# Pairing row blocks 0 and 1 in the second mixing layer of an FNet + GEGLU kernel

## The chip, the cores and the metric

The kernel runs on one core of a Trainium2 chip (trn2). The metric is the device time of one execution in microseconds (us). TensorE (PE in the profile) does the matrix products, VectorE (DVE) and ScalarE (ACT) the elementwise work, GpSimd (POOL) and SyncE (SP) mostly issue DMAs. Hardware behaviour is told here as the traces of this case show it.

## The reference

Four residual layers work on an activation `x` of 2048 rows by 512 columns, in float32. Layers 0 and 2 mix, layers 1 and 3 are a gated feed-forward network:

```
def mix(x):                     # x: 2048 x 512
    a = x @ dft_hid_re.T
    b = x @ dft_hid_im.T
    return dft_seq_re @ a - dft_seq_im @ b

def ffn(x):
    return (gelu(x @ w_gate) * (x @ w_up)) @ w_down     # 1792 hidden columns

x = x + mix(layernorm(x)); x = x + ffn(layernorm(x))    # layers 0 and 1
x = x + mix(layernorm(x)); x = x + ffn(layernorm(x))    # layers 2 and 3
```

All weights are inputs that don't change between the layers: layers 0 and 2 use the same sequence matrices.

## The kernel before

**Products.** A float32 tile is split into a high and a low part (`split`, L122: ACT copies the high part in a rounded type at L124, DVE subtracts it from the source at L126), and one product of tiles is three matrix instructions, high by high, high by low and low by high (`mm3`, L162, lines 164 to 166), summed in PSUM. Each has a 128x128 stationary and a 128x512 moving operand. In the feed-forward layers and in the sequence product of the mixing layers, the matrices are divided into two by two blocks and multiplied in Winograd's form of Strassen's algorithm: seven block products (A11, A12, S1, S2, S3, S4, A22 by their left operand) in place of eight, for sums and differences of blocks that DVE makes (`minus` L151, `plus` L154).

**The mixing layers** (`mix`, L711) multiply the sequence matrices with the normalized rows first, for four row blocks `b` of 512 output rows (`NB` is 4), and the hidden matrices then. `plan` (L403) writes out the order of a layer's stages. Layer 0 begins with the first two products of all four row blocks in one pass (`fore`); layer 2 does them one row block after the other (`a11`, `a12`). They are followed, for each row block, by stages S2 (`s2`, L823: three block products, 8 steps each) and S4 (`s4`, L859: two block products). A step (`six`, L752) takes one tile of the sequence matrices and issues six matrix instructions. The results of a row block are eight tiles of sums, `cs`. Then one of two things is done with the hidden matrices:

- `hid_groups` (L729): eight groups of twelve matrix instructions, in three parts that lie between and behind S2 and S4 (`EARLY_HID`, `MID_HID`, `LATE_HID`). Residual rows are added in `x_add` (L204). This is 96 instructions for a row block.
- `pair_products` (L897): two row blocks together are a two by two problem and are multiplied in Winograd's form: seven products of four tiles (`PAIR_ORDER`, L401) by six instructions, 168 for both. `pair_member` (L885) collects the sums of both and loads their residual rows into two wide tiles (`load_turned`, L227); `prepared` (L902) makes the block sums and splits, `LEAD_PAIR` (4) products ahead; `ended` (L926) adds a finished product to the wide tiles (`turned_rows`, L234: a transpose and an addition on DVE) and stores rows (`rows_done`, L244, four DMAs on POOL). The block sums of the hidden matrices for it (`whd`, L262) are made in layer 1.

`PAIRED` (L43) says which row blocks begin a pair: in layer 2 only block 2 (with 3). Blocks 0 and 1 of layer 2, and all of layer 0, go through `hid_groups`.

**The stream.** Every tile of a matrix that is needed in order is an item of `items` (L286). `take` (L315) hands out the next; it splits items up to `AHEAD` (7) before their use, and `split_next` (L308) loads up to `RAW` (6) items before that, all by DMAs of SP. In stage S2 an item loads three tiles of the sequence matrix, and `make_s2` (L345) makes S1, S2 and S3 of them on DVE; S1 and S3 are split by later items, S2 is kept until `make_s4` (L367) has made S4 with it.

**Slots.** Tiles live in 93 slots of 128x512 (`Slots`, L83; `sb.get` and `sb.put`). Two wide tiles, "x" and "z", are lent to the slots as four more each when they are free (`lend` L170, `reclaim` L109); in layer 2 "z" is taken back in S4 of block 0 and "x" in S4 of the block that begins a pair, and nothing may lie in a lent slot when `load_turned` takes the wide tile (L230).

**Other work** is queued: `step` (L486) runs one entry of `queue` after each step of products, and an entry of None is a pause. `chores_at(b)` (L714) is such work for the next layer: for b = 1 and 2 it normalizes the rows of blocks 0 and 1 for layer 3, which it reads back from memory (`x_load_mixed`, L195, four DMAs of SP for 128 rows), and for b = 2 in layer 0 it also makes weights. The scheduler of the framework then sets each engine's order of instructions from a model of the times.

**Start and end.** `WARM` (12, L29) products of an identity matrix (L1320) are issued before the first data; each is two records in the trace. `last_rows` (L1247) does the last block product of the kernel in two cuts of 256 columns, and after each cut it stores four pieces, each issued on an engine of a list (L1253).

Of the kernel before, what the change touches and what calls it, by code (L numbers as in the profile page):

```python
# [9 lines left out]
F32 = mybir.dt.float32  # L10
# [4 lines left out]
P = 128  # L15
# [4 lines left out]
TB = 512  # L20
NB = S // TB
# [6 lines left out]
RAW = 6  # L28
WARM = 12  # L29
OPEN_MORE = 0  # L30
# [10 lines left out]
CUT = 256  # L41
KEEP22 = {0: (2, 3), 2: ()}
PAIRED = {0: (), 2: (2,)}  # L43
NEAR_PAIR = 8
LEAD_PAIR = 4
WHD_AT = 6
BACK_AT = 4, 7
KEEP_AT = 2
# [11 lines left out]
def fnet_geglu(ctx: ExitStack, tc: tile.TileContext, x_in, ws, wh, whc, wgu, wdc, out):  # L60
# [22 lines left out]
    class Slots:  # L83


        def __init__(self, pool, name, n):
            self.pool, self.name, self.free, self.held = pool, name, list(range(n)), {}
            self.least, self.lent = n, set()

        def get(self, dtype=F32):  # L90
            at = next(i for i, n in enumerate(self.free) if dtype == F32 or isinstance(n, int))
            n = self.free.pop(at)
            self.least = min(self.least, len(self.free))
            t = self.pool.tile([P, 512], dtype, name=f"{self.name}{n}") if isinstance(n, int) else n[0]
            self.held[id(t)] = (n, t)
            return t
# [59 lines left out]

    def copied(src):
        v = sb.get()
        nc.scalar.activation(v, src, AF.Copy)  # L159
        return v  # L160
# [92 lines left out]

    def fetched(key):
        t = sb.get()
        nc.sync.dma_start(t, away.pop(key))
        return t
# [86 lines left out]

    def make_s2(k, keep):  # L345
        def run(a21, a22, *a11):
            a11 = a11[0] if a11 else held.pop(k)
            s1 = a22
            if keep:
                held["A22", k], s1 = a22, sb.get()  # L350
            plus(s1, a21, a22)
            minus(a21, a11, a21)
            minus(a11, s1, a11)
            s1s[k], s2s[k], s3s[k] = s1, a11, a21
            return split_slot(a11)
        return run
# [9 lines left out]

    def make_s4(k):  # L367
        def run(a12):
            v = s2s.pop(k)
            minus(a12, a12, v)  # L370
            sb.put(v)
            return plain(a12)
        return run
# [59 lines left out]
    def mix_items(layer):  # L433
# [3 lines left out]
        for b, what in plan(layer):  # L437
# [14 lines left out]
            elif what == "S2":  # L452
                for i, k in skewed(3):
                    if i == 0:
                        raw(make_s2(k, b in KEEP22[layer]), a21[k], a22[k], *(() if hold else (a11[k],)))
                    else:
                        raw(make_s1(k) if i == 1 else make_s3(k))
            elif what == "S4":
                for i, k in skewed(2):
                    if i == 0:  # L460
                        raw(make_s4(k), a12[k])
                    elif b in KEEP22[layer]:
                        raw(make_a22(k))
                    else:
                        raw(plain, a22[k])
# [245 lines left out]
    def mix(layer):  # L711
        hid, sums, chores, hid_left = {}, {}, [], [0]

        def chores_at(b):  # L714
# [46 lines left out]
        def based(b, c, ps):  # L761

            if b >= FORE[layer]:
                return copied(ps)
            v = sb.get()
            plus(v, sums[b][c], ps)
            return v
# [11 lines left out]
        def a12(b):  # L779
# [4 lines left out]
            for c in range(2):  # L784
                v = sums[b][c]
                if b < FORE[layer]:
                    t = sb.get()
# [35 lines left out]
        def s2(b):  # L823
# [10 lines left out]
            for i, k in skewed(3):  # L834
                if b and fore and i == 0 and k == (0 if layer else BACK_AT[0]):
                    sums[b] = [fetched((layer, b, c)) for c in range(2)]
                if b and fore and i == 0 and k == (0 if layer else BACK_AT[1]):
                    cs.update({(0, c): fetched((layer, b, c, "sum")) for c in range(2)})
                if i == 0:
# [12 lines left out]
                for c in range(2):  # L852
                    if i == 1:
                        v = cs[1, 2 + c] = sb.get()
                        plus(v, us[b][c], one[c])
# [3 lines left out]
        def s4(b):  # L859
# [7 lines left out]
            for i, k in skewed(2):  # L867
# [6 lines left out]
                for c in range(2):  # L874
                    if i == 0:
                        v = cs[0, 2 + c] = sb.get()
                        plus(v, u[c], one[c])
# [7 lines left out]
        def pair_member(b):  # L885

            if b in PAIRED[layer]:
                pair.update({(0, key): cs.pop(key) for key in list(cs)})
                queue.extend([run for chore in chores_at(b) for run in (chore, None)])
            elif b - 1 in PAIRED[layer]:  # L890
# [6 lines left out]
        def pair_products(b):  # L897

            bs, ys, banks, seconds = {}, {}, {}, {}
            chores.extend(chores_at(b))  # L900

# [45 lines left out]
            for i, (name, k) in enumerate(PAIR_ORDER):  # L947
# [113 lines left out]
    def geglu(w, layer):  # L1061
# [185 lines left out]
        def last_rows():  # L1247
# [216 lines left out]
```

## Time and profile before

| What | Value |
|---|---|
| Median of 3 runs | 1597.19 us (1595.58 to 1597.57) |
| The profiled execution's own time | 1594.87 us |
| Its span, first to last instruction | 1593.1 us |
| Outside the span | 1.77 us |
| TensorE's mean granted clock | 0.999 |
| TensorE busy | 1585.2 us |
| VectorE busy | 1245.9 us |
| ScalarE busy | 865.0 us |
| GpSimd busy | 233.4 us |
| DMA | 418.66 MB, mean 263 GB/s |

The profiled execution is one run. It was 2.32 us below the median of the three timed runs, so a sum over its rows gives a difference, and the difference is carried over to the median. Busy times are shares of one engine's own line; TensorE's are of matrix instructions that overlap (each shows 388 ns on average, but one starts well before the one ahead of it has ended), so the distance between starts is what one instruction costs.

The times of the stages can be read off by counting matrix instructions along TensorE's line. Layer 0 lies at about 6.5 to 398 us: the common pass to 94, then 76 us for each row block, so that block 2 has 246 to 322 us. Layer 1 lies at 398 to 798 us, layer 2 at 798 to 1184: the first products to 885, blocks 0 and 1 at 885 to 961 and 961 to 1037, S2 and S4 of blocks 2 and 3 at 1037 to 1146, their pair at 1146 to 1184. Layer 3 takes the rest. The scheduler lets neighbouring stages overlap a little, so these bounds are rough.

### The profile page before, as it was taken

Reading aid. Unit: us, or ns where it says so; the run is one execution under the profiler, and the core shown is the slowest. Engines: PE = TensorE matmul, PEld = TensorE weight load, DVE = VectorE, ACT = ScalarE, POOL = GpSimd, SP = SyncE. Lnnn points to the kernel's source line nnn. Section 1 sums busy time; section 2 is a strip of 40 time slices with the busy share of each in tenths; the row PEclk is TensorE's granted clock in tenths of the full one; section 3 lists DMA queues with packets and bytes.
Section 4 is the critical chain, followed back from the end, with each engine's and each line's share of the span. In section 5 each row is a group of like instructions: output and inputs, shape, how many; then the busy total and the mean of one; then the engine's idle time right before and its main releaser. Section 6 shows DMA issues by size and latency. Waiting matters only on the chain.

```text
span 1593.1 us, 23069 instructions
## 1 busy us (share of the span) xinstructions
PE 1585.2 (100%) x7026; PEld 1313.6 (82%) x7026; DVE 1245.9 (78%) x2164; ACT 865.0 (54%) x1696; POOL 233.4 (15%) x410
## 2 busy tenths in 40 slices
PE   9999999999999999999999999999999999999998
PEld 8888888888888888888888888888888888888887
DVE  8999989798799794666869978788985458754475
ACT  7864565544766653656767535446446435433361
POOL 2200311302455201230031000001002000000000
PEclk9999999999999999999999999999999999999999
DMA  9946967897999989995867687768998967896452
GB/s 361 332 146 231 376 225 240 285 300 256 327 344 337 307 304 300 313 338 200 298 225 253 233 272 250 238 228 248 271 352 237 285 201 237 298 282 200 137 191 55
DMA packets 249500, 418.66 MB, mean 263 GB/s; under 512 B 28608, under 2 KB 81856, under 8 KB 248352
## 3 DMA queue, kind: packets, MB, share of 16 engines
q1 hardware_dynamic: 224720, 334.07, 65.5%
q0 software_dynamic: 23840, 82.73, 14.2%
q8 instruction: 56, 0.92, 0.2%
q10 hardware_dynamic: 816, 0.39, 0.1%
q14 instruction: 68, 0.56, 0.1%
HBM read 335.54 MB, written 81.53 MB: 262 GB/s over the span
## 4 chain that ended last, share of the span: by engine, by line
PE 85%; issue 11%; DMA 3%; SPq 0%; POOL 0%; ACT 0%; POOLq 0%; DVE 0%
PE p L164 28%; PE p L165 28%; PE p L166 28%; DMA s<-ws 1%; DMA s<-wb 1%; DMA wide<-x 1%; DMA out<-wide 0%; POOL out L245 0%; SPq L300 0%; SPq L232 0%; SPq L192 0%; SPq L1048 0%; ACT s L124 0%; ACT s L556 0%; POOLq L1460 0%
## 5 line engine op out<-in xcount | busy, mean ns | idle before, releaser
L165 PE MATMUL p<-s,s 128*128 128x512 f32 (+1 forms) x2334 | 902.7, 388 | 0.0
L166 PE MATMUL p<-s,s 128*128 128x512 f32 (+1 forms) x2334 | 890.8, 388 | 0.0
L164 PE MATMUL p<-s,s 128*128 128x512 f32 (+1 forms) x2334 | 879.5, 388 | 0.2 <-ACT s L124 0.2
L124 ACT ACTIVATE s<-s 128x512 fp32r<-128x512 f32 (+1 forms) x848 | 476.6, 607 | 326.1 <-DVE s L152 112.9
L126 DVE TENSOR_TENSOR s<-s,s 128x512 fp32r<-128x512 f32 (+1 forms) x848 | 531.8, 662 | 56.7 <-ACT s L124 49.3
L164 PEld LDWEIGHTS p<-s,s 128*128 128x128 f32 x2334 | 438.4, 188 | 91.4 <-ACT s L124 1.4
L165 PEld LDWEIGHTS p<-s,s 128*128 128x128 f32 x2334 | 438.4, 188 | 90.4 <-DVE s L126 0.6
L166 PEld LDWEIGHTS p<-s,s 128*128 128x128 f32 x2334 | 438.2, 188 | 89.9 <-DVE s L126 0.3
L155 DVE TENSOR_TENSOR s<-s,p 128x512 f32<-128x512 f32 x284 | 190.8, 683 | 195.0 <-PE p L166 111.8
L152 DVE TENSOR_TENSOR s<-s,s 128x512 f32<-128x512 f32 (+1 forms) x411 | 246.9, 617 | 4.8 <-DMA s<-ws 2.5
L159 ACT ACTIVATE s<-p 128x512 f32<-128x512 f32 x246 | 143.7, 592 | 144.8 <-PE p L166 140.2
L1058 ACT ACTIVATE s<-s 128x512 f32<-128x512 f32 x112 | 70.4, 629 | 120.5 <-DVE s L155 110.2
L283 POOL DMA_DIRECT2D wb<-s x84 | 46.0, 549 | 118.9 <-ACT s L124 81.9
L124 ACT ACTIVATE s<-xwide 128x512 fp32r<-128x512 f32 (+1 forms) x68 | 41.0, 616 | 34.9 <-DVE xwide L155 7.2
L1072 DVE TENSOR_TENSOR s<-s,s 128x512 f32<-128x512 f32 x84 | 57.8, 689 | 1.9
L126 DVE TENSOR_TENSOR s<-xwide,s 128x512 fp32r<-128x512 f32 (+1 forms) x68 | 45.2, 676 | 6.9 <-ACT s L124 6.9
L556 ACT ACTIVATE s<-s,shift,rstd 128x512 f32<-128x512 f32 x54 | 43.1, 807 | 4.1 <-DVE shift L520 4.0
L245 POOL DMA_DIRECT2D out<-wide x8 | 5.2, 657 | 271.6 <-DVE wide L155 181.0
L155 DVE TENSOR_TENSOR s<-s,s 128x512 f32<-128x512 f32 (+1 forms) x70 | 41.0, 588 | 4.9 <-DMA s<-ws 3.2
L283 POOL DMA_DIRECT2D wc<-s x42 | 30.3, 723 | 73.3 <-ACT s L124 50.6
L529 POOL TENSOR_SCALAR rstd<-rstd 128x1 f32<-128x1 f32 x48 | 12.8, 268 | 191.3 <-ACT junk L528 190.4
L245 POOL DMA_DIRECT2D x<-wide x12 | 7.9, 662 | 215.3 <-DVE wide L155 214.4
(107 smaller groups left out, 530.7 us busy)
## 6 DMA issues: line engine op xcount, KB each, us to landing
s<-ws SPq DMA_DIRECT2D x367, 256.0 KB, 4.9
s<-wb SPq DMA_DIRECT2D x294, 256.0 KB, 5.3
s<-wc SPq DMA_DIRECT2D x196, 256.0 KB, 4.5
wb<-s POOLq DMA_DIRECT2D x98, 256.0 KB, 5.0
s<-wh SPq DMA_DIRECT2D x64, 256.0 KB, 4.8
s<-x SPq DMA_DIRECT2D x53, 256.0 KB, 5.2
xwide<-ws SPq DMA_DIRECT2D x49, 256.0 KB, 4.1
wc<-s POOLq DMA_DIRECT2D x49, 256.0 KB, 5.3
```

The lines of the kernel that those rows point to most:

```text
L124: nc.scalar.activation(hi, src, AF.Copy)
L126: nc.vector.tensor_tensor(lo, src, f32(hi), op=ALU.subtract)
L152: nc.vector.tensor_tensor(out, a, b, op=ALU.subtract)
L155: nc.vector.tensor_tensor(out, a, b, op=ALU.add)
L159: nc.scalar.activation(v, src, AF.Copy)
L164: nc.tensor.matmul(ps, ah, bh, start=start, stop=False, skip_group_check=True)
L165: nc.tensor.matmul(ps, ah, bl, start=False, stop=False, skip_group_check=True)
L166: nc.tensor.matmul(ps, al, bh, start=False, stop=stop, skip_group_check=True)
L283: nc.gpsimd.dma_start(to, t)
L556: nc.scalar.activation(z, x, AF.Identity, bias=shift, scale=rstd)
L1058: nc.scalar.activation(t, g, AF.Gelu_apprx_tanh)
L1072: nc.vector.tensor_tensor(t, t, v, op=ALU.mult)
```

## The change

Row blocks 0 and 1 of layer 2 become a pair as well, so the stages of the layer are now S2 and S4 of blocks 0 and 1, their pair, S2 and S4 of blocks 2 and 3, and their pair. While a layer has block 0 in a pair, the tiles of sums (`cs` and what leads to them) are taken from the 93 own slots only and never from lent ones (`own=True` and `strict`), and the wide tile "x" is taken back in S4 of block 0. The work for layer 3 that used to lie in the hidden products of block 1, and behind S4 of block 2, is queued behind the first pair, 6 pauses first (`PAIR_WAIT`) and 3 pauses after each entry (`PAIR_GAP`).

The sequence matrices are the same in layers 0 and 2, so layer 0 now also writes the block sums S1, S2, S3 and S4 of row block 2 to memory (`stored_for`: 4 tiles for each of 8 steps, 32 DMAs of 256 KB on POOL's queue), and layer 2 reads them there: stages S2 and S4 of block 2 load as many tiles as before and have no sums to make.

One warming product goes, and the lists of issuing engines of the two last cuts are exchanged in part.

```diff
-WARM = 12
+WARM = 11
...
-PAIRED = {0: (), 2: (2,)}
+PAIRED = {0: (), 2: (0, 2)}
+PAIR_GAP = 3
+PAIR_WAIT = 6
+STORED = 2,
...
-            self.least, self.lent = n, set()
+            self.least, self.lent, self.strict = n, set(), False
...
-            at = next(i for i, n in enumerate(self.free) if dtype == F32 or isinstance(n, int))
+            at = next(i for i, n in enumerate(self.free) if dtype == F32 and not (own and self.strict) or isinstance(n, int))
...
+    stored = {(b, k, n): dram.tile([P, 512], F32, name=f"{n}_{b}_{k}") for b in STORED for k in range(NK) for n in ("S1", "S2", "S3", "S4")}
+
+    def stored_for(b, k, **tiles):
+
+        if b in STORED:
+            for name, t in tiles.items():
+                nc.gpsimd.dma_start(stored[b, k, name], t)
...
             s1s[k], s2s[k], s3s[k] = s1, a11, a21
+            stored_for(b, k, S1=s1, S2=a11, S3=a21)
             return split_slot(a11)
...
             minus(a12, a12, v)
+            stored_for(b, k, S4=a12)
...
-                    if i == 0:
-                        raw(make_s2(k, b in KEEP22[layer]), a21[k], a22[k], *(() if hold else (a11[k],)))
+                    if layer and b in STORED:
+                        raw(plain, stored[b, k, ("S2", "S1", "S3")[i]])
+                    elif i == 0:
+                        raw(make_s2(b, k, b in KEEP22[layer]), a21[k], a22[k], *(() if hold else (a11[k],)))
...
-                    if i == 0:
-                        raw(make_s4(k), a12[k])
+                    if i == 0 and layer and b in STORED:
+                        raw(plain, stored[b, k, "S4"])
+                    elif i == 0:
+                        raw(make_s4(b, k), a12[k])
...
+        sb.strict = 0 in PAIRED[layer]
...
                 pair.update({(0, key): cs.pop(key) for key in list(cs)})
-                queue.extend([run for chore in chores_at(b) for run in (chore, None)])
+                if 0 not in PAIRED[layer]:
+                    queue.extend([run for chore in chores_at(b) for run in (chore, None)])
...
-            chores.extend(chores_at(b))
+            if b == NB - 1:
+                chores.extend(chores_at(b))
...
+            if b == 1:
+                queue.extend([None] * PAIR_WAIT + [run for at in (1, 2) for chore in chores_at(at) for run in (chore, *[None] * PAIR_GAP)])
...
-            for cut, engines in ((slice(0, CUT), (nc.sync, nc.scalar)), (slice(CUT, TB), (nc.sync, nc.scalar, nc.gpsimd))):
+            for cut, engines in ((slice(0, CUT), (nc.gpsimd, nc.sync, nc.scalar)), (slice(CUT, TB), (nc.sync, nc.scalar))):
```

The other edits pass `own=True` where the tiles of sums are made (`copied`, `based`, `fetched`, `a12`, `s2`, `s4`).

More of the change, by code (lines that the diff above doesn't have):

```diff
@@ L87, in __init__, with get @@
             self.pool, self.name, self.free, self.held = pool, name, list(range(n)), {}
-            self.least, self.lent = n, set()
-        def get(self, dtype=F32):
-            at = next(i for i, n in enumerate(self.free) if dtype == F32 or isinstance(n, int))
+            self.least, self.lent, self.strict = n, set(), False
+        def get(self, dtype=F32, own=False):
+            at = next(i for i, n in enumerate(self.free) if dtype == F32 and not (own and self.strict) or isinstance(n, int))
             n = self.free.pop(at)
@@ L155, in plus, with copied @@
         nc.vector.tensor_tensor(out, a, b, op=ALU.add)
-    def copied(src):
-        v = sb.get()
+    def copied(src, own=False):
+        v = sb.get(own=own)
         nc.scalar.activation(v, src, AF.Copy)
@@ L252, in put_away, with fetched @@
         sb.put(t)
-    def fetched(key):
-        t = sb.get()
+    def fetched(key, own=False):
+        t = sb.get(own=own)
         nc.sync.dma_start(t, away.pop(key))
@@ L343, in make_a11, with make_s2 @@
         return run
-    def make_s2(k, keep):
+    stored = {(b, k, n): dram.tile([P, 512], F32, name=f"{n}_{b}_{k}") for b in STORED for k in range(NK) for n in ("S1", "S2", "S3", "S4")}
[3 more added lines that the diff above has]
+                nc.gpsimd.dma_start(stored[b, k, name], t)
+    def make_s2(b, k, keep):
         def run(a21, a22, *a11):
@@ L365, in make_s3, with make_s4 @@
         return lambda: plain(s3s.pop(k))
-    def make_s4(k):
+    def make_s4(b, k):
         def run(a12):
@@ L763, in based @@
             if b >= FORE[layer]:
-                return copied(ps)
-            v = sb.get()
+                return copied(ps, True)
+            v = sb.get(own=True)
             plus(v, sums[b][c], ps)
@@ L786, in a12 @@
                 if b < FORE[layer]:
-                    t = sb.get()
+                    t = sb.get(own=True)
                     plus(t, v, side[c])
@@ L837, in s2 @@
                 if b and fore and i == 0 and k == (0 if layer else BACK_AT[1]):
-                    cs.update({(0, c): fetched((layer, b, c, "sum")) for c in range(2)})
+                    cs.update({(0, c): fetched((layer, b, c, "sum"), True) for c in range(2)})
                 if i == 0:
@@ L853, in s2 @@
                     if i == 1:
-                        v = cs[1, 2 + c] = sb.get()
+                        v = cs[1, 2 + c] = sb.get(own=True)
                         plus(v, us[b][c], one[c])
@@ L875, in s4 @@
                     if i == 0:
-                        v = cs[0, 2 + c] = sb.get()
+                        v = cs[0, 2 + c] = sb.get(own=True)
                         plus(v, u[c], one[c])
```

## The prediction

> **What bounds the kernel now.** I read the page first, then TensorE's groups by shape, its waits and a piece of its timeline, then the windows of the stages, and the two ends last. The page:
>
> ```profile
> span 1593.1 us, 23069 instructions
> PE 1585.2 (100%) x7026; PEld 1313.6 (82%) x7026; DVE 1245.9 (78%) x2164; ACT 865.0 (54%) x1696; POOL 233.4 (15%) x410
> DVE  8999989798799794666869978788985458754475
> ```
>
> TensorE is busy in 1585.2 of 1593.1 us. Busy alone does not prove the bound, since the records overlap, so the waits come next:
>
> ```profile
> PE p L1321 <- POOL ident masks.py:199: 1.4, 1, 1.4
> PE p L164 <- ACT s L124: 0.2, 1, 0.2
> ```
>
> These two rows are all that TensorE waited for: 1.4 us ahead of the warming products and 0.2 us once later. Two rows of its timeline, with 43 starts from the one to the other, give its pace:
>
> ```profile
> 1043.14 0.39 PE L165 MATMUL p<-s,s 128*128 128x512 f32 x1
> ...
> 1052.88 0.39 PE L164 MATMUL p<-s,s 128*128 128x512 f32 x1
> ```
>
> (1052.88 - 1043.14) / 43 = 0.2265 us from start to start. The groups by shape say how many there are (the other two lines of `mm3` have 2306 as well):
>
> ```profile
> L165 PE MATMUL p<-s,s 128*128 128x512 f32 x2306 | 894.8, 389 | 0.0
> ```
>
> 3 x 2306 x 0.2265 = 1567 us: the span is this count times this pace, with some 26 us of warming, narrower products, small waits and ends. One wide matrix instruction less is worth 0.2265 us as long as nothing else comes to bound. The windows show what could: their columns are the stretch, its length, the busy time of PE, PEld, DVE, ACT and POOL, the granted clock, the DMA share and GB/s.
>
> ```profile
> 6.50:94.00 87.50, 87.29 (x383) 71.70 (x383) 84.85 (x202) 70.55 (x134) 15.93 (x23) 1.00 0.90 323
> 246.00:322.00 76.00, 76.00 (x337) 62.94 (x336) 65.49 (x112) 43.18 (x86) 20.09 (x37) 1.00 0.80 277
> 885.00:1037.00 152.00, 152.00 (x672) 125.91 (x671) 127.44 (x208) 67.10 (x127) 6.37 (x14) 1.00 0.74 249
> 1146.00:1184.00 38.00, 38.00 (x169) 31.46 (x169) 38.00 (x65) 19.02 (x34) 0.00 (x0) 1.00 1.05 346
> ```
>
> The reader is to see that TensorE is full in every stage, that VectorE is full as well in the pair (38.00 of 38.00), and that the DMA engines are full there too (share 1.05).
>
> **The change, part by part.**
>
> *Products.* Blocks 0 and 1 lose 2 x 96 = 192 instructions of `hid_groups` and gain 7 x 4 x 6 = 168 of the same 128x512 shape. 24 x 0.2265 = **5.44 us** off the engine that sets the end. The clock in all windows is 1.00, so no other pace is to be expected.
>
> *VectorE at the pair.* A pair costs DVE 16 differences, 28 splits, 6 additions and 8 transposes with 8 additions: 66 instructions. The splits of the stream's next 7 items fall beside it too: 73. DVE's own pace, from two rows of its timeline:
>
> ```profile
> 1164.57 3.09 DVE L126 TENSOR_TENSOR s<-s,s 128x512 fp32r<-128x512 f32 x5
> 1167.58 0.68 DVE L148 SCALAR_TENSOR_TENSOR s<-s,s 128x512 fp32r<-128x512 f32 x1
> ```
>
> 3.01 / 5 = 0.602 us each. 73 x 0.602 = 43.9 us stand against 168 x 0.2265 = 38.1 us of products, 5.9 us more. The stretch ahead has to bring that as a lead. S2 and S4 of one block are this window:
>
> ```profile
> 1037.00:1092.00 55.00, 55.00 (x244) 45.56 (x243) 48.80 (x80) 22.92 (x40) 2.24 (x4) 1.00 0.67 214
> ```
>
> 80 x 0.602 = 48.2 us against 240 x 0.2265 = 54.4 us. Over both blocks and the pair DVE has 2 x 48.2 + 43.9 = 140.3 us to do in 2 x 54.4 + 38.1 = 146.9 us, 96%. The window 6.5 to 94 had 84.85 of 87.50, 97%, and TensorE lost 0.2 us there; the pair of blocks 2 and 3 had DVE at 100% and TensorE lost nothing. In the pair's own order the work just fits: the last tile's products begin 6 instructions ahead of the end, at 36.7 us, DVE owes 62 instructions (37.3 us) by then, and the first five tiles are prepared before the pair begins. I take **0**, with 5.9 us as the other end if no lead exists. Below nothing is excluded, since TensorE can't go under its count. Behind the pair, block 2 is lighter than before: its 32 sums are gone (32 x 0.602 = 19.3 us of DVE), which pays for the transposes of the norms moved there. As TensorE bounds, that relief is worth nothing of itself.
>
> *Stores in layer 0.* 32 x 256 KB = 8.39 MB more on POOL's queue in block 2's 76 us. What moves there now, from the DMA view of 246 to 322 us (the second row has 40 slices):
>
> ```profile
> GB/s 218 182 415 365 106 172 229 57 157 279 354 376 273 202 298 260 352 430 224 170 209 212 317 303 364 396 410 418 406 424 223 272 197 396 111 41 235 223 432 361
> DMA packets 9727, 21.04 MB, mean 277 GB/s; under 512 B 1408, under 2 KB 1920, under 8 KB 9465
> ...
> q1 hardware_dynamic: 7673, 13.10, 54.1%
> q0 software_dynamic: 2048, 7.87, 26.0%
> ...
> s<-ws SPq DMA_DIRECT2D x24, 256.0 KB, 5.2
> wh<-s POOLq DMA_DIRECT2D x16, 256.0 KB, 5.8
> ```
>
> ```profile
> L283 POOL DMA_DIRECT2D wh<-s x16 | 9.0, 561 | 33.0 <-ACT s L124 14.0 <-ACT mean L527 10.8 <-DVE s L126 7.9
> ```
>
> 21.04 + 8.39 = 29.43 MB. At the 418 GB/s that single slices reach this takes 70.4 us of the 76; at the 346 GB/s mean of the pair's window it takes 85.1, 9.1 us too many. The traffic that TensorE needs is SP's, 13.10 MB or 172 GB/s, under half of either rate; the stores only hold slots longer, by the 5.8 us to landing of POOL's other stores. I take **0** and keep 9.1 us as the other end. The Trainium skill, "DMA: Bandwidth & Descriptors", section "Where 436 GB/s comes from", says that the side of the HBM, about 358 GB/s, binds such transfers; by it the 29.43 MB would take 82.2 us, 6.2 too many (an estimate from that page), and the trace speaks against it with nine slices over 390 GB/s. The stores' issue is about 32 x 0.561 = 18 us (the last row's mean) on a POOL that is busy for 20.09 of 76 us; behind them wait only its small norm steps and other stores.
>
> *Work for layer 3, and SP's queue.* Rows of block 0 leave last: four DVE instructions (2.4 us), four stores on POOL, their landing. The nearest rows are those stores in layer 3 and their landing, and what SP has waited for rows so far:
>
> ```profile
> 1387.06 2.63 POOL L245 DMA_DIRECT2D out<-wide  x4 [90.65 <-DMA s<-wb]
> ```
>
> ```profile
> DMA to landing us min/median/max: 3.7/6.6/7.9
> ```
>
> ```profile
> SPq L201 <- DMA x<-wide: 9.0, 3, 6.8
> ```
>
> 2.4 + 2.6 + 7.9 = 12.9 us after the pair's last product; the six pauses last 6 x 6 x 0.2265 = 8.2 us. SP can stand for 4.7 us, with the stream's loads queued behind it. Those run up to 7 + 6 = 13 items ahead, 13 x 6 x 0.2265 = 17.7 us, and SP stood 6.8 us for this reason before while TensorE waited for none. **0**; up to 4.7 if the lead is used up.
>
> *Slots.* Eight sums of block 0 stay through block 1's S2 and S4, and the four slots of "x" are gone there. Loads then start later, since they wait for a slot. That stretch shows such waits already, as DVE waiting for a load:
>
> ```profile
> DVE s L155 <- DMA s<-ws: 7.0, 2, 3.8
> ```
>
> It ended no wait of TensorE, so **0**; where these 7.0 us come on top of DVE's 140.3, it is 0.4 us over its 146.9, and its part is in the rival below. The hidden products' loads (32 tiles) give way to 28 tiles, which changes little.
>
> *Start.* The identity products and the chain of waits at the start:
>
> ```profile
> 1.35 5.49 PE L1321 MATMUL p<-ident 128*128 128x128 f32 x24 [1.35 <-POOL ident masks.py:199]
> ```
>
> ```profile
> 4.49 5.13 DMA s<-ws
> 9.64 5.40 DMA s<-ws
> 15.06 5.39 DMA s<-ws
> ...
> 23.64 0.50 PE p L164
> ```
>
> A product less frees TensorE 5.49 / 12 = 0.46 us earlier. But the chain up to 23.64 us is one of loads, so the first products only wait longer there: **0**, at most 0.46 gained.
>
> *End.* The last cut's stores:
>
> ```profile
> 1587.78 0.84 SPq L1263 DMA_DIRECT2D out<-xwide  x2
> 1587.78 0.37 ACTq L1263 DMA_DIRECT2D out<-xwide  x1
> 1588.04 0.58 POOL L1263 DMA_DIRECT2D out<-xwide  x1 [5.32 <-DVE xwide L155]
> ```
>
> ```profile
> out<-xwide SPq DMA_DIRECT2D x2, 128.0 KB, 2.7
> out<-xwide ACTq DMA_DIRECT2D x1, 128.0 KB, 2.9
> out<-xwide POOLq DMA_DIRECT2D x1, 128.0 KB, 3.4
> ```
>
> POOL's lands last, at 1588.04 + 3.4 = 1591.4. In its place ACT issues a second one at 1587.78 + 0.37 = 1588.15, landing near 1591.1. **0.3 us** gained; from 0 to 0.5.
>
> Sum against the profiled execution: 1594.87 - 5.44 - 0.3 = 1589.1 us (a span near 1587.4). The median of the runs shown is 2.32 us above that execution; from it, 1597.19 - 5.7 = **1591.5 us**.
>
> **The rivals.**
>
> 1. *VectorE becomes the bound at the first pair.* Without a lead the pair loses up to 5.9 us: 1591.5 + 5.9 = 1597.4; half of it gives 1594.4. For it: 96% over 147 us without a break, where the hidden products of block 0 (96 instructions in 21.7 us beside 12 of DVE in 7.2) used to give DVE time to catch up, and tighter slots. Against it: the pair of blocks 2 and 3, into which 22 instructions of the next layer's work are queued as well (14 splits, 8 differences), ran without a loss.
> 2. *The stores fill the DMA engines in layer 0* (slower than before). If 346 GB/s is all there is and the loads share the delay, TensorE ends block 2 up to 9.1 us late: 1591.5 + 9.1 = 1600.6. It decides against the change from a delay of 5.7 us on. For it: the pair's window with share 1.05. Against it: loads need 172 GB/s, and the highest slices show room. The figure of the Trainium skill named above (358 GB/s, "DMA: Bandwidth & Descriptors") is the milder form of this rival: with 6.2 us it would end at 1597.7, an estimate from that page, and its chance is within this rival's.
> 3. *SP's queue stands for the rows of block 0*, 4.7 us: 1596.2. Against it: the 6.8 us stood before without a loss.
> 4. *The change doesn't do what it says*: the 24 instructions go, but the time passes to a wait that comes due later, at the head of layer 3, since its norms now begin a pair later. They still end in block 2, with block 3 and a pair (about 92 us) ahead of layer 3, so I give it no price of its own.
>
> **How the numbers follow.** The forecast has 0.75, rival 1 0.13, rival 2 0.06, rival 3 with what remains 0.06. About 0.2% (3.2 us) is what a measurement here can tell from no change, so faster means below 1594.0. The forecast lies there; of rival 1, evenly spread from 0 to 5.9 us, about 0.4 (0.05) does. Rivals 1 and 3 give same for the rest (0.14), rival 2 slower in most of its cases (0.05), same in the others. Faster 0.80, same 0.15, slower 0.05. The range: downwards the start's 0.46 and the end's other 0.2, and the 1.6 us by which the fastest of the three runs lies under the median, 1591.5 - 2.3 = 1589.2; upwards to the part of rival 1 up to 3.5 us, 1595.0. That leaves out the worst of rivals 1 and 3 and rival 2, under 2 in 10.
>
> **What would show it.** Right: 24 fewer wide instructions (8 fewer in each of the three lines), the same 0.2265 us pace, TensorE's waits still under 1 us beside the start, the last landing a few tenths earlier behind the last product. Rival 1: TensorE waits for DVE's L126 or L148 near 1000 to 1035 us. Rival 2: waits for loads or splits at 250 to 330 us, with loads taking well over 5.2 us to land. Rival 3: SP waiting for `x<-wide` at about 1040 us and TensorE with it. The prediction is wrong if any of these adds more than 2.5 us.

## The result, and the profile after

The changed kernel takes 1590.96 us (median of 6 runs, 1590.40 to 1592.87), the kernel before 1596.51 (6 runs, 1595.58 to 1597.57): a ratio of 0.9968 with a 95% interval of 0.9958 to 0.9979, 5.5 us less. Forecast were 1591.5 and 5.7 us less. Against the larger set of runs of before that came with the experiments (28 runs, median 1595.93) it is 5.0 us less. The interval of the ratio says how well the saving is known: it lies between 3.4 and 6.7 us.

The page of the changed kernel, the lines that answer to those of before:

```profile
span 1589.3 us, 23178 instructions
PE 1579.5 (99%) x7000; PEld 1308.4 (82%) x7000; DVE 1249.1 (79%) x2174; ACT 875.8 (55%) x1714; POOL 252.5 (16%) x443
DVE  8999989889799795566969997868985458754475
```

Line numbers moved: L164 to L166 are L167 to L169 now, the split's L124 and L126 are L127 and L129, `minus` and `plus` are L155 and L158. One of the three lines of `mm3` in the groups by shape, and all that TensorE waited for:

```profile
L168 PE MATMUL p<-s,s 128*128 128x512 f32 x2298 | 891.1, 389 | 1.2 <-DVE s L129 1.2
```

```profile
PE p L1343 <- POOL ident masks.py:199: 1.3, 1, 1.3
PE p L168 <- DVE s L129: 1.2, 1, 1.2
PE p L167 <- ACT s L127: 1.2, 3, 0.5
```

2298 stands where 2306 stood: 3 x 8 = 24 instructions fewer, as counted. But the last two rows are new: 2.4 us of waits, where before had 0.2. Of them 0.9 lie in the common pass of layer 0, the others at 919 and 1101 us. The prediction had named waits under 1 us as a sign of being right, and this sign is not met. The windows of the stages that the change touched, with the columns of the earlier fence:

```profile
246.00:322.00 76.00, 76.00 (x337) 62.94 (x336) 64.73 (x111) 43.32 (x86) 28.73 (x54) 1.00 0.98 350
...
994.00:1032.00 38.00, 38.00 (x169) 31.48 (x168) 33.88 (x57) 19.21 (x35) 0.00 (x0) 1.00 0.77 242
1032.00:1086.00 54.00, 54.00 (x240) 44.72 (x239) 36.81 (x62) 39.17 (x90) 13.23 (x25) 1.00 0.95 290
1086.00:1140.00 54.00, 52.78 (x233) 43.38 (x232) 53.97 (x91) 27.82 (x49) 1.13 (x2) 1.00 0.97 279
```

The rows are layer 0's block 2, and in layer 2 the first pair, S2 and S4 of block 2, and S2 and S4 of block 3. The reader is to see three things. The DMA share of layer 0's block 2 went from 0.80 to 0.98. VectorE isn't full in the new pair (33.88 of 38). It is full in block 3 (53.97 of 54), and there TensorE has its one wait of some length: it stands idle for 1.22 us and loses about 1.5 us of its pace.

The difference of the two profiled executions adds up. The spans differ by 3.8 us. 24 x 0.2265 = 5.4 less for the products; 0.4 less between the end of the last product and the end of the span (6.3 before, 5.9 after); 0.5 more up to the end of layer 0's common pass; 1.5 more for the time lost behind it, at 919 us (0.6) and 1101 us (1.5) against 0.6 in all before: -5.4 - 0.4 + 0.5 + 1.5 = -3.8. The medians differ by more because the profiled execution of before, 1594.87, lies below all six timed ones.

### The profile page after: what moved, and what is told of

Same layout as the page of the kernel before. It is cut to its first block, busy times and chain, and to the rows that moved or that the text cites. A ratio compares the mean times of both kernels' runs of the same rounds, so it can differ in the third digit from the quotient of the medians.

```text
span 1589.3 us, 23178 instructions
## 1 busy us (share of the span) xinstructions
PE 1579.5 (99%) x7000; PEld 1308.4 (82%) x7000; DVE 1249.1 (79%) x2174; ACT 875.8 (55%) x1714; POOL 252.5 (16%) x443
## 4 chain that ended last, share of the span: by engine, by line
PE 97%; DMA 1%; DVE 1%; SPq 0%; issue 0%; ACT 0%; POOL 0%; DVEq 0%; ACTq 0%
PE p L168 32%; PE p L167 32%; PE p L169 32%; DMA s<-ws 1%; DVE s L129 0%; ACT s L127 0%; DVE s L155 0%; SPq L303 0%; SPq L195 0%; ACT s L573 0%; DVE wide L155 0%; DVE s L158 0%; DVE xwide L155 0%; POOL rstd L536 0%; DVE s L242 0%
## 5 line engine op out<-in xcount | busy, mean ns | idle before, releaser
L168 PE MATMUL p<-s,s 128*128 128x512 f32 x2326 | 899.0, 388 | 1.2 <-DVE s L129 1.2
L169 PE MATMUL p<-s,s 128*128 128x512 f32 x2326 | 887.4, 388 | 0.0
L167 PE MATMUL p<-s,s 128*128 128x512 f32 x2326 | 871.6, 388 | 1.3 <-ACT s L127 1.2
L127 ACT ACTIVATE s<-s 128x512 fp32r<-128x512 f32 (+1 forms) x868 | 487.6, 608 | 319.3 <-DVE s L155 110.7
L129 DVE TENSOR_TENSOR s<-s,s 128x512 fp32r<-128x512 f32 (+1 forms) x868 | 543.7, 664 | 56.7 <-ACT s L127 52.0
L167 PEld LDWEIGHTS p<-s,s 128*128 128x128 f32 x2326 | 436.6, 188 | 93.1 <-ACT s L127 3.6
L169 PEld LDWEIGHTS p<-s,s 128*128 128x128 f32 x2326 | 436.8, 188 | 89.5
L158 DVE TENSOR_TENSOR s<-s,p 128x512 f32<-128x512 f32 x289 | 194.1, 683 | 196.5 <-PE p L169 119.0
L155 DVE TENSOR_TENSOR s<-s,s 128x512 f32<-128x512 f32 (+1 forms) x414 | 248.5, 619 | 2.9 <-DMA s<-ws 1.0
L127 ACT ACTIVATE s<-xwide 128x512 fp32r<-128x512 f32 (+1 forms) x52 | 31.0, 614 | 26.8 <-DVE xwide L158 10.5
L158 DVE TENSOR_TENSOR s<-s,s 128x512 f32<-128x512 f32 (+1 forms) x68 | 39.9, 587 | 4.7 <-DMA s<-wgu 2.6
L129 DVE TENSOR_TENSOR s<-xwide,s 128x512 fp32r<-128x512 f32 (+1 forms) x52 | 34.7, 675 | 5.9 <-ACT s L127 5.7
```

Source lines behind the costliest of these rows:

```text
L127: nc.scalar.activation(hi, src, AF.Copy)
L129: nc.vector.tensor_tensor(lo, src, f32(hi), op=ALU.subtract)
L155: nc.vector.tensor_tensor(out, a, b, op=ALU.subtract)
L158: nc.vector.tensor_tensor(out, a, b, op=ALU.add)
L167: nc.tensor.matmul(ps, ah, bh, start=start, stop=False, skip_group_check=True)
L168: nc.tensor.matmul(ps, ah, bl, start=False, stop=False, skip_group_check=True)
```

## The experiments

The theory to test was the prediction's: the saving is TensorE's count times its pace, and everything else is hidden. Its rivals were VectorE at the first pair, the stores in layer 0, and the wait for the rows of block 0. "Against the change" below is the difference of a kernel's ratio and the change's 0.9968, times 1596 us; each ratio's interval is about 0.001 (1.6 us) to either side, so such a difference is known to about 2.2 us.

One thing has to be known to read the profiles that follow. Each is one execution, and executions differ in stages that no edit touched. Count TensorE's products from the start, and compare the time of the one that begins at 885 us in the change, behind the first products of layer 2. It comes at the same time in `dve24`, 0.8 us later in `more24`, 1.1 in `store_only`, 1.5 in `gap0`, 1.6 in `gap2`, 2.0 in `hole`, 2.4 in `less24`, 2.7 in `no_store`, 2.8 in `dve32_b2` and 3.7 in `hole2`. In the kernels among these whose edit lies in layer 2 behind this point (all but `store_only` and `no_store`), every engine has the same operations on the same tiles in the same order up to there, buffer numbers apart, so a new order by the scheduler is not the cause; what is stays open. "In place" below means that this part is taken off the profile's difference.

### Are the 24 products the saving?

`store_only` takes the first pair back and keeps the rest of the change:

```diff
-PAIRED = {0: (), 2: (0, 2)}
+PAIRED = {0: (), 2: (2,)}
```

> The changed kernel without the first pair (blocks 0 and 1 go through the hidden products again), with stores, one warming product less and the exchanged ends kept. The 24 instructions are back: if they are the gain, 1591.0 + 5.4 = 1596.4, 0.3 under the time before at most. If the gain came from the stored sums or the ends instead, it stays near 1591.

Measured: 1595.33 us, ratio 0.9996 (0.9987 to 1.0005): 4.5 us against the change. The stores, the relief of block 2, the ends and the warming alone are worth nothing that can be told from no change; the saving is the pair's. The profile has a little over 3 us in place: 5.4 for the products, less what the change loses at 919 and 1101 us (0.6 and 1.5) and `store_only` doesn't.

`more24` adds 24 instructions of the same shape to the first pair:

```diff
+                if b == 1 and name != "A22":
+                    spare = ps8.get()
+                    nc.tensor.matmul(spare, hi, parts[0], start=True, stop=True, skip_group_check=True)
+                    ps8.put(spare)
```

> The changed kernel with 24 more matrix instructions of 128x512 in the first pair (one behind each product of A11, A12, S1, S2, S4 and S3, into a spare PSUM bank that nobody reads). If TensorE's count times its pace is the whole of the gain, they cost 24 x 0.2265 = 5.4 us: 1591.0 + 5.4 = 1596.4, the time before. If another engine sets the pace at the first pair (VectorE, by rival 1), the extra instructions fall into its gaps and the time stays at 1591 to 1593.

Measured: 1596.80 us, ratio 1.0008 (1.0000 to 1.0017): 6.4 us against the change, 0.27 us for each instruction where 0.2265 were expected, within the interval. TensorE sets the pace of the pair in this direction. The wait at 1101 us is gone from the profile of `more24`: products that come later find their operands ready.

`less24` leaves 24 out (the high by low instruction of the first 128 columns in six products of the first pair):

```diff
-    def mm3(ps, a, b, start, stop):
+    def mm3(ps, a, b, start, stop, short=False):
...
-        nc.tensor.matmul(ps, ah, bl, start=False, stop=False, skip_group_check=True)
+        if not short:
+            nc.tensor.matmul(ps, ah, bl, start=False, stop=False, skip_group_check=True)
...
-                    mm3(banks[bank][c], (hi, lo), parts, ...)
+                    mm3(banks[bank][c], (hi, lo), parts, ..., b == 1 and name != "A22" and c == 0)
```

> The changed kernel, where six of the first pair's seven block products leave out the high by low instruction of their first 128 columns (24 matrix instructions; the result loses that part). If only TensorE's count matters, 1591.0 - 5.4 = 1585.6. By the budget of the prediction VectorE then has 140.3 us of work in 141.5 us of products, so the count still decides, just. If VectorE already sets the pace of the first pair, nothing is gained: 1590 to 1591.

Measured: 1592.49 us, ratio 0.9982 (0.9973 to 0.9991): 2.2 us against the change, which can't be told from no difference; the 5.4 us didn't come off. In the other direction the rule ends at once. TensorE's timeline at the head of block 3 in `less24` shows where they went; the number in brackets is the idle time ahead. (This execution took 1595.55 us, the longest of the kernel's eleven.)

```profile
1097.10 0.39 PE L170 MATMUL p<-s,s 128*128 128x512 f32 x1
1100.57 1.22 PE L167 MATMUL p<-s,s 128*128 128x512 f32 x2 [3.08 <-ACT s L127]
1104.46 0.80 PE L169 MATMUL p<-s,s 128*128 128x512 f32 x1 [2.67 <-DVE s L129]
1105.05 0.63 PE L170 MATMUL p<-s,s 128*128 128x512 f32 x1
1105.48 0.63 PE L169 MATMUL p<-s,s 128*128 128x512 f32 x1
1105.91 0.63 PE L170 MATMUL p<-s,s 128*128 128x512 f32 x1
...
```

There is no wait at the pair (990 to 1030 us had DVE at 36.19 of 40). It comes some 70 us later, at the same place where the changed kernel waits for 1.2 us: products that arrive earlier only wait longer there. The wait then costs more than itself, since the next products start 0.43 us apart (1105.05, 1105.48, 1105.91), twice the usual distance. Of this run's time 2.4 us lie in layer 0, nearly all at 181 to 196 us, where the order of work is that of the change. In place the profile is 1.9 us over the change in spite of its 24 products less.

### What are the stored sums for?

`no_store` undoes the stores and lets block 2 make its own sums again:

```diff
-STORED = 2,
+STORED = ()
```

> The changed kernel with the stores of block sums undone (STORED empty): layer 0 writes 8.4 MB less, and block 2 of layer 2 makes its 32 sums on VectorE again, beside the moved norms. If both are hidden, as predicted, the time is that of the change: 1591.0, within 1.5. If the stores cost time in layer 0 (rival 2), it is faster, 1585 to 1589. If the pairing needs VectorE's relief in block 2, it is slower: 32 x 0.602 = 19.3 us more work, of which 54.4 - 48.2 - 5 = about 1 us finds room beyond what was free, so up to some us, 1593 to 1600, with waits of TensorE for splits in block 2.

Measured: 1601.77 us, ratio 1.0035 (1.0023 to 1.0047): 10.7 us against the change, slower than before, and 1.8 us above the range expected. The head of block 2 in this kernel, and behind the change's row TensorE's longest waits in it:

```profile
1032.00:1068.00 36.00, 35.65 (x157) 29.00 (x156) 36.00 (x61) 16.76 (x32) 7.35 (x9) 1.00 0.71 212
```

The same window of the changed kernel:

```profile
1032.00:1068.00 36.00, 36.00 (x161) 29.80 (x160) 22.95 (x39) 23.55 (x51) 8.93 (x16) 1.00 0.88 291
```

```profile
PE p L167 <- ACT s L127: 4.6, 6, 2.9
PE p L167 <- DVE s L158: 3.3, 1, 3.3
```

VectorE is busy in 36.00 of 36.00 us where the change has 22.95, and TensorE stops at 1069 to 1073 and 1130 to 1134 us. In place this profile lies 8.5 us behind the change's. That is more than the 5.4 us of the products, so without the relief the pairing is a loss.

`dve32_b2` tells whether VectorE's work did that, or the slots and the order of loads. It keeps the stored sums, and adds 32 additions on VectorE, one ahead of each split:

```diff
+    def plain_and_more(v):
+        spare = ps8.get()
+        plus(spare, v, v)
+        ps8.put(spare)
+        return plain(v)
...
-                        raw(plain, stored[b, k, ("S2", "S1", "S3")[i]])
+                        raw(plain_and_more, stored[b, k, ("S2", "S1", "S3")[i]])
...
-                        raw(plain, stored[b, k, "S4"])
+                        raw(plain_and_more, stored[b, k, "S4"])
```

> The changed kernel with its stored block sums kept, and 32 additions of 128x512 more on VectorE in block 2 of layer 2, one ahead of the split of each stored tile (into a spare PSUM bank that nobody reads). That is VectorE's work of the run without stores, without that run's slots for the kept sums and without its loads of three tiles at a time. If it was VectorE's work that made that run 10.8 us slower, this one is at 1599 to 1603 with waits at 1065 to 1080 us and near 1100 to 1130. If it was slots or the order of loads, VectorE's idle time in block 2 takes most of it: 1591 to 1595.

Measured: 1602.68 us, ratio 1.0039 (1.0026 to 1.0053): 11.3 us against the change. The profile lies 8.6 us behind the change's in place, against 8.5 in `no_store`, so VectorE's work alone accounts for it. (Each addition also takes a spare PSUM bank, which `no_store` doesn't; that both lose the same speaks against the bank.) Its window reads as that of the run without stores:

```profile
1030.00:1070.00 40.00, 40.00 (x177) 32.84 (x175) 40.00 (x68) 19.48 (x42) 11.19 (x12) 1.00 0.84 268
```

`dve24` adds 24 additions in the pair instead:

```diff
+                if b == 1 and name in ("A11", "A12", "S1", "S2", "S4", "S3"):
+                    spare = ps8.get()
+                    plus(spare, f32(parts[0]), f32(parts[0]))
+                    ps8.put(spare)
```

> The changed kernel with 24 additions of 128x512 more on VectorE in the first pair (one behind each product but A22's, into a spare PSUM bank that nobody reads): 24 x 0.602 = 14.4 us. If VectorE is the bound there or has just no slack (rival 1), most of it comes through: 1600 to 1605. If it has the slack that the profile shows (33.9 busy of 38.0 in the pair, then 9.25 us idle in block 2), about 14.4 - 4.1 minus a lead of up to 6.8 = 3.5 us come through: 1593 to 1596.

Measured: 1603.62 us, ratio 1.0044 (1.0032 to 1.0057): 12.1 us against the change for 14.4 us of work. The range for "no slack" was met, but not its place. (The profile shows 10.3 us, all of it in place.) TensorE's waits in this kernel:

```profile
PE p L167 <- ACT s L127: 6.5, 4, 5.4
PE p L168 <- DVE s L129: 2.1, 2, 1.6
```

The pair itself lost 0.6 us (at 1032 us); the long ones come behind the products of 1101.7 and 1108.1 us, again the head of block 3, with slow products for some 6 us behind them. So from the first pair to the head of block 3 VectorE's work is one budget, and it has no room left, although VectorE idles in it. What it idles for shows in its waits between 1032 and 1110 us in the changed kernel:

```profile
DVE s L158 <- PE p L169: 11.7, 3, 9.2
DVE wide L664 <- DMA t<-wide: 4.1, 1, 4.1
```

The 9.2 us end at 1059.7: the next instruction in VectorE's order is an addition that needs a finished product of block 2, and all that stands behind it in the order waits too. How much of that was ready isn't shown. The 4.1 us end at 1084.5: a transpose for layer 3 has to wait until the wide tile that it writes to has been stored.

### How much room do the stores have?

`stores_twice` writes each block sum of block 2 to two places:

```diff
+    again = {key: dram.tile([P, 512], F32, name="again_" + "_".join(map(str, key))) for key in stored}
...
-                nc.gpsimd.dma_start(stored[b, k, name], t)
+                for to in (stored, again):
+                    nc.gpsimd.dma_start(to[b, k, name], t)
```

> The changed kernel, where layer 0 writes each block sum of block 2 twice (to two places), 8.4 MB more on POOL's queue. If stores are hidden, as the prediction has it, 1591, within 1.5. If the DMA engines are the limit (rival 2), 37.8 MB in block 2 take 90 us at 418 GB/s, 14 us over its 76, and part of that comes through: 1595 or more, with waits at 250 to 330 us.

Measured: 1606.63 us, ratio 1.0062 (1.0048 to 1.0075): 15.0 us against the change, with waits at 302 to 329 us. `stored23` stores, and uses, the sums of block 3 too:

```diff
-STORED = 2,
+STORED = 2, 3
```

> The changed kernel, where layer 0 stores the block sums of row blocks 2 and 3 both, and layer 2 reads them for both. The run without stores was 10.8 us slower than the change and waits for splits at the head of blocks 2 and 3, so the theory now is that VectorE and the loads, not TensorE alone, bound S2 of block 3, where the moved norms end. By it the 32 sums less in block 3 take away the 1.4 us wait at 1101 us: 1589 to 1590, if 8.4 MB more in layer 0 are hidden. If stores aren't hidden (rival 2), they cost in layer 0's block 3: over 1592.

Measured: 1603.23 us, ratio 1.0046 (1.0034 to 1.0059): 12.4 us against the change. Half of the theory held: from the first products of layer 2 to the last of the kernel it takes 1.9 us less than the change, as the wait at 1101 us is gone and most of that at 919. But layer 0 takes 12.5 us more, in one wait at 352 us with slow products behind it. The rows of the kernel that stored twice come first, then those of `stored23` (the window ahead of its wait, and the two waits in it):

```profile
246.00:302.00 56.00, 55.90 (x247) 45.97 (x246) 41.62 (x69) 27.14 (x53) 30.01 (x57) 1.00 1.03 405
302.00:335.00 33.00, 23.82 (x78) 17.39 (x78) 24.47 (x42) 16.44 (x35) 11.89 (x23) 0.79 0.88 328
```

```profile
322.00:351.00 29.00, 29.00 (x129) 24.03 (x128) 20.09 (x33) 8.60 (x15) 10.25 (x19) 1.00 0.99 383
```

```profile
PE p L167 <- ACT s L127: 10.0, 1, 10.0
...
DVE s L155 <- DMA s<-ws: 8.4, 2, 5.8
```

TensorE's 10.0 us go back to VectorE's sums, and these waited for sequence tiles. The DMA engines carried 405 GB/s over 56 us, so the 346 GB/s of the prediction is no limit, and a full queue does no harm for a while: TensorE lost 0.1 us in those 56. That it stops when the lead of the loads is used up is the reading that fits; what delayed each load wasn't followed up. The DMA view for the change, 246 to 322 us, against 21.04 MB, 7.87 MB of POOL's queue and 5.2 us to landing before:

```profile
DMA packets 11409, 26.59 MB, mean 350 GB/s; under 512 B 1744, under 2 KB 2256, under 8 KB 11146
...
q0 software_dynamic: 3764, 13.45, 44.0%
...
s<-ws SPq DMA_DIRECT2D x25, 256.0 KB, 6.4
```

The loads took 1.2 us more to land in the change, and it cost nothing; in `stores_twice` they took 7.7, and it cost 15 us. (VectorE runs ahead of TensorE, so 14 of the changed kernel's 32 stores are issued before this window, from 225 us on: 26.59 MB moved in it, not the 29.43 of the prediction.)

### What do the pauses keep apart?

`gap0` queues the work for layer 3 right behind the pair:

```diff
-PAIR_GAP = 3
-PAIR_WAIT = 6
+PAIR_GAP = 0
+PAIR_WAIT = 0
```

> The changed kernel without the 6 pauses and the 3 pauses after each entry, so that the reading and normalizing of rows for layer 3 is queued right behind the first pair. If it is rival 3's wait (SP standing for the rows of block 0, stream loads behind it) that the pauses avoid, TensorE waits in block 2 and the time rises by up to the 12.9 us that the rows need: 1593 to 1600. If the stream's lead covers that, the transposes come earlier into VectorE's idle time of block 2 (9.25 us at 1050 to 1060), the wait at 1101 goes, and the time is 1589.5 to 1591.

Measured: 1614.67 us, ratio 1.0116 (1.0102 to 1.0130): 23.6 us against the change, far above the range expected. TensorE waits 11.1 us at 1055 us and again at 1077 to 1086. The expectation named the rows of block 0 as what is late, rightly, but put the wait on SP's queue. SP waited 4.4 us for them; ScalarE's timeline shows the rest:

```profile
1050.52 0.63 ACT L127 ACTIVATE s<-s 128x512 fp32r<-128x512 f32 x1 [4.92 <-DMA s<-ws]
1060.83 0.63 ACT L543 ACTIVATE junk<-s 128x512 f32<-128x512 f32 x1 [9.68 <-DMA s<-x]
...
1066.08 0.61 ACT L127 ACTIVATE s<-s 128x512 fp32r<-128x512 f32 x1
```

L543 is the first instruction of a norm. ScalarE stood 9.68 us for its rows, and from 1050.5 to 1066.1 us it made no split, for which TensorE waited.

`gap2` shortens only the later pauses:

```diff
-PAIR_GAP = 3
+PAIR_GAP = 2
```

> The changed kernel with 2 pauses after each entry of the layer 3 work in place of 3 (the first 6 pauses stay). Everything from the second norm on is queued 1 to 8 steps (1.4 to 10.9 us) earlier. If the spare time of VectorE in block 2 is what is missing at the head of block 3, the wait at 1101 us (1.5) goes: 1589.5. If the rows come too late for the earlier norms, as without any pause (there ScalarE stood 9.7 us for rows and held up the splits), it is slower: 1592 to 1600.

Measured: 1607.33 us, ratio 1.0069 (1.0057 to 1.0082): 16.1 us against the change, above the range expected too. One pause less in each place, and ScalarE waits 4.4 us for rows (L543) and TensorE 4.6 us for its split; a second wait of some 4 us follows at 1133. Two more kernels set the pauses one by one, to take away VectorE's 4.1 us wait for the wide tile. `hole` and `hole2` are the same edit with other numbers:

```diff
-PAIR_GAP = 3
+PAIR_GAPS = 2, 2, 2, 2, 6, 3, 3, 3, 3        # hole
+PAIR_GAPS = 3, 3, 3, 3, 5, 2, 2, 2, 2        # hole2
...
-                queue.extend([None] * PAIR_WAIT + [run for at in (1, 2) for chore in chores_at(at) for run in (chore, *[None] * PAIR_GAP)])
+                queue.extend([None] * PAIR_WAIT + [run for chore, gap in zip(chores_at(1) + chores_at(2), PAIR_GAPS, strict=True) for run in (chore, *[None] * gap)])
```

> The changed kernel with 2 pauses after the first four entries, 6 after the fifth and 3 after the others: the sixth entry, whose transpose must wait until the first wide tile is written (the 4.1 us that VectorE waits at 1080 to 1084), keeps its place, while the write that it waits for is issued 4 steps earlier. If that wait is what makes VectorE late at the head of block 3, the 1.5 us at 1101 go: 1589.5. If the earlier norms meet rows that are not there yet, 1592 or more.

Measured: 1596.95 us, ratio 1.0005 (0.9996 to 1.0013): 5.9 us against the change, 2.4 in place in the profile; ScalarE stood 6.8 us for rows here, against 1.8 in the change.

> The changed kernel with 3 pauses after the first four entries as in the change, 5 after the fifth and 2 after the others: the sixth entry is queued 2 steps (2.7 us) later, the last one 1 step earlier. If VectorE's 4.1 us wait for the write of the wide tile is what makes it late at the head of block 3, 2.7 of them go and with them the wait at 1101: 1589.5 to 1590. If VectorE's sum of work up to there counts, and not this wait, it stays 1591.

Measured: 1593.96 us over a wide spread (1591.15 to 1599.20), ratio 0.9989 (0.9979 to 0.9999): 3.4 us against the change; neither expectation was met. The wait for the wide tile did shrink:

```profile
DVE wide L664 <- DMA t<-wide: 0.9, 1, 0.9
```

and the wait at 1101 us is gone from that profile. But 1.0 us came up at 1125 us. In place the profile gains 0.4 us on the change; 3.7 us were lost ahead of the edit. That local waits can be removed is shown; that it pays is not. None of the kernels tried beats the change.

## Why the prediction was right, and where it was not

**Products: right.** 24 instructions at 0.2265 us. The pair taken back costs 4.5 us, 24 more cost 6.4; the forecast's 5.4 lies between. That 5.7 us were forecast and 5.5 measured is luck in part. In the profiles the pair brings 2.1 us of waits that the forecast put at nothing, and the whole is 3.8 us; the medians have 5.0 to 5.5, in an interval that holds both.

**VectorE at the first pair: 0 was right, the budget's end was not.** The pair ran without a wait, as the sum of 140.3 us in 146.9 said; the profile has 134.24 in 147.00:

```profile
885.00:1032.00 147.00, 146.65 (x647) 121.13 (x646) 134.24 (x221) 67.58 (x117) 1.08 (x2) 1.00 0.72 221
```

But the sum was closed at the pair's last product. The runs with 24 instructions more on VectorE or 24 fewer on TensorE show that the work is carried on to the head of block 3, where the moved norms end, and that no room is left there. Rival 1 named the right engine and gave it the wrong place, at 1000 to 1035 us in place of 1101. Rival 4 had the kind of it, a wait that comes due later, and expected it at the head of layer 3, where TensorE waits for nothing; it came at the head of block 3.

**"That relief is worth nothing of itself": true to the letter, wrong as a price.** This is the step to correct. The prediction said that the relief of 19.3 us pays for the norms' transposes, and then put it at nothing, as VectorE is off the path. Taken alone it is worth nothing (`store_only`). But without it the kernel is 10.7 us slower than the change, 8.5 in place, and 5.6 us slower than before (1.0035); with the relief kept and the same work put back it loses as much. So the pairing needs it. The norms that the change moves into block 2 are a likely part of the reason; no run moved them away alone, so their share isn't shown. The forecast came out right because the change contains both.

**Stores in layer 0: 0 was right, with less room than argued.** The stores went through at a share of 0.98 in block 2's window and no wait, and blocks 2 and 3 of layer 0 take no less in `no_store`, which leaves them out. That loads need under half of the rate was no sound argument: in `stores_twice` SP's queue moved about the same 13 MB in 246 to 333 us, but each load took 7.7 us, and TensorE stopped. The Trainium skill's 358 GB/s ("DMA: Bandwidth & Descriptors", section "Where 436 GB/s comes from") isn't what binds here; 405 GB/s over 56 us stand against it. Rival 2 lies not far off: between 8.4 MB of stores, which cost nothing, and 16.8, which cost 15 us, it takes over.

**The rows of block 0: 0 was right for the pauses as set,** and the forecast bore them out as needed. SP stood 2.0 us for rows at 1030 to 1062 us, and TensorE didn't wait. The queue that matters is ScalarE's, which makes the splits, and not only SP's: without pauses the price was 23.6 us, where the prediction had the rows ready 12.9 us behind the pair.

**Start and end.** The start gained nothing, as said (the profile has it 0.5 us later, with a wait of 0.45 us at 12.6). The end gained 0.4 for 0.3: no piece of the last cut goes out over POOL, and the pieces of both engines land about 3 us after their issue:

```profile
1584.40 0.85 SPq L1285 DMA_DIRECT2D out<-xwide  x2
1584.40 0.89 ACTq L1285 DMA_DIRECT2D out<-xwide  x2
```

```profile
out<-xwide SPq DMA_DIRECT2D x2, 128.0 KB, 2.9
out<-xwide ACTq DMA_DIRECT2D x2, 128.0 KB, 3.1
```

**Open.** What the own slots for the sums are worth was not tried: without them a sum can lie in the wide tile that `load_turned` needs. The wait near 920 us, in block 0, stands in most profiles with the first pair and in neither `store_only` nor before, so it seems to come with the pairing; but `less24` and `stores_twice` have the pair and no such wait, and which part brings it wasn't followed up.

## What to carry to other kernels

When one engine is full, count what is taken off it, and that is the most that can be saved; then read the other engines' budgets up to the point where all the moved work ends, not to the end of the stage that was changed. An edit that looks free because its engine is off the path may be what keeps it off: undo it by itself before calling it worthless. And a kernel without a wait says nothing about how far the next wait is: a second kernel with a known load of 8 MB or 24 instructions more, or with some taken off, tells it. Two profiles are compared stage by stage, since stages that nobody touched differ by up to 3.7 us here.

## What the runs showed of the hardware

TensorE is slow after a long wait. Behind all waits of 2.9 us and more but one (3.25 us, in `no_store`) products start about 0.43 us apart, for some 3 to 6 us, which adds 1.5 to 3.3 us to the wait itself. The granted clock shows it: it was 0.79 at 302 to 335 us of `stores_twice`, and 0.75 at 1090 to 1110 us of `less24`, where it fell from full to half:

```profile
1090.00:1110.00 20.00, 14.26 (x49) 10.76 (x48) 17.98 (x31) 8.58 (x15) 0.62 (x1) 0.75 0.98 310
```

```profile
1097.50:1100.00 2.50, 0.00 (x0) 0.00 (x0) 2.29 (x4) 0.72 (x3) 0.00 (x0) 0.99 1.05 380
1100.10:1110.10 10.00, 6.86 (x15) 4.98 (x16) 8.29 (x14) 3.90 (x7) 0.00 (x0) 0.50 0.91 232
```

Single waits of up to 1.9 us (1.2 in the change, 1.9 in `hole`) left the pace at 0.227. The Trainium skill ("TensorE: Matmul & The Clock Gate", section "What's actually happening") tells of a clock that is halved after about 3.4 us without work; the trace agrees on the half, with 0.50 and 0.43 for 0.227 us, but not on the time: in `less24` the clock fell about 2.5 us after TensorE's last product had ended.

The DMA engines held 405 GB/s over 56 us (`stores_twice`), and the change's 32 stores cost TensorE nothing at a share of 0.98 in 76 us.
